# A bias row of its own for every query tile in a forgetting attention: one VectorE instruction per score block

## The chip, the cores and the metric

The kernel runs on one core of one Trainium2 chip. The time is that of the device in microseconds (us), from the first to the last instruction of the program; three runs of the kernel before gave 919.32, 919.80 and 922.17 us.

The engines are named as in the profile: PE is TensorE's matmul and PEld its weight load, DVE is VectorE, ACT is ScalarE, POOL is GpSimd, SP is SyncE, which here issues every transfer.

## The reference, cut to what matters

Eight batches of eight heads, 576 positions, 64 wide. Attention has a forgetting bias, and its output feeds a channel mix.

```python
scores = q @ k.T / sqrt(D)
cum    = cumsum(maximum(s, 0), axis=-1)
bias   = -(cum[..., :, None] - cum[..., None, :])
scores = where(causal, -1e9, scores + minimum(bias, 0))      # causal: key after query
attn   = exp(scores - max(scores)); attn = attn / (sum(attn) + 1e-9)
x      = heads side by side of attn @ v                      # [B, S, 512]
# channel mix, per position, with x_prev the position before
xk = mu_k * x + (1 - mu_k) * x_prev;  xr = mu_r * x + (1 - mu_r) * x_prev
k  = maximum(xk @ w_k, 0);  out = sigmoid(xr @ w_r) * (k * k @ w_v)
```

Within a row of scores the part of the bias that belongs to the query is a constant, and softmax does not see it. So the kernel adds only `cum` of the key, scaled by 8 (the root of D), to the raw product, the same row for every query of a head. Keys after the query get a very large negative number instead.

## The kernel before, in words

**Attention.** The 576 queries of a head are cut into five tiles: the first has 64 queries, the others 128. Tile t sees the keys up to its own last query, so its scores are 64, 192, 320, 448 and 576 columns wide (`KN`), and only the last 64 or 128 of them, from `QS[t]` on, hold keys that some query must not see. Batch 0 is done in halves so that the channel mix can begin early: `A` is tiles 0 to 2, `Z` tiles 3 and 4, for each of its four pairs of heads; from batch 1 on a visit does all five tiles (`ALL`) of a pair of heads.

`prefix_sums` puts the running sums of all 64 heads into DRAM (`cum_d`). `scores` (line 625) does one head: one transfer on SP (line 630) spreads the head's row over 128 partitions into `CB`, one of two buffers. Two selects on POOL (line 649) copy the columns that need a mask from `CB` to `M`, also one of two buffers, with the masked keys replaced: one select for the 64 columns of tile 0, one for the masked blocks of all other tiles at once. The first two heads take their rows from `first_sums`, which computes them on the spot.

For each tile `products` (line 661) makes two matmuls into one of two score banks of PSUM (line 678), and VectorE (line 693) adds the bias, scales, writes the scores to `W` and keeps the row's minimum of the negated scores in `nm`. It shows as two instructions: the pass (CUSTOM_DVE_ANT_0) and the read of the accumulator into `nm`. A tile takes two of them, the second continuing from the minimum of the first: the columns ahead of `QS[t]` with `CB`, the masked block with `M`. Tile 0 has only the masked block. Tile 4 is wider than a bank and comes as two halves of 288 columns: the first needs one pass, the second two (160 columns, then 128). ScalarE then takes exponentials and their sums (line 711), POOL normalizes (line 724), and `weighted` (line 758) transposes the weights on TensorE (line 770), copies them out with their rests (lines 797, 801, 829, 836, 844) and multiplies with the values (line 903).

Every product of 32-bit numbers is done as a rounded part and a rest. The splits of keys and queries are casts on ScalarE (lines 603, 614) and subtractions on POOL (lines 607, 618, 563), those of the weights of the channel mix lines 507 to 538.

**Channel mix.** 18 chunks of 256 positions (`channel_mix`, line 958): the mix of x and its predecessor on ScalarE and VectorE (lines 979, 988, 1007, 1011), the hidden layer (line 1040, and lines 1052 to 1069 for the square), the gate (line 1082) and the output (line 1107). The gate's result lies in one of two buffers with the tag `g`, 512 columns wide.

**The order.** No queue's order is written by hand. `Plan` collects every instruction as a task with an engine, an estimated cost, what it depends on and a due time, and simulates the five engines: on each engine the ready task that is due first goes next. It does so eight times, with due times worked back from the last simulation, keeps the shortest, and emits the instructions in that order. So the order on each queue follows from the estimated costs of all tasks; the engines then run their queues strictly in order. A buffer taken from `sbuf(shape, tag, n)` is one of n places in turn, and its tasks depend on all tasks of the place's last user. A select costs 137 ns plus 0.83 ns per column in the plan, a score pass 68 ns plus 1.04 ns per column, a transfer at least 520 ns on SP.

Of the kernel before, what the change touches and what calls it, by code (L numbers as in the profile page):

```python
# [285 lines left out]
def forgetting_attention_then_channel_mix(  # L286
# [15 lines left out]
    nc = tc.nc  # L302

    B, H, D, S = q.shape
    DM, DF = moe_w_k.shape
    P = 128
# [18 lines left out]
    def sbuf(shape, tag, bufs=1, dtype=F32):  # L325
        return plan.buffer(sb, shape, dtype, tag, bufs)

    def bank(n, tag, bufs=1):
        return plan.buffer(psum, [P, 512 * n], F32, tag, bufs)

    def fixed(t):
        b = Buffer(lambda: t)
        b.ap = t
        return b
# [7 lines left out]
    def act(emit, reads, writes, n, extra=51, table=0):  # L342
        return plan.add("ACT", n * 0.8333 + extra, emit, reads, writes, land=table)

    def dve(emit, reads, writes, n, rate=0.96):
        return plan.add("DVE", n / rate + 68, emit, reads, writes)

    def pool(emit, reads, writes, n, extra, rate=0.8333):
        return plan.add("POOL", n * rate + extra, emit, reads, writes)

    def dma(emit, reads, writes, ns):
        return plan.add("SP", max(520, ns), emit, reads, writes, land=1300)
# [13 lines left out]
    QS = [0] + [64 + P * t for t in range(NQ - 1)]  # L366
    QN = [64] + [P] * (NQ - 1)
    KN = [QS[t] + QN[t] for t in range(NQ)]
# [43 lines left out]
    cum_d = fixed(dram.tile([B * H, S], F32, name="cum_d"))  # L412
# [26 lines left out]
    def first_sums(nk):  # L439

        raw = sbuf([P, 2, nk], "raw", 4)
        ones = sbuf([P, nk], "raw", 4)
        cbs = [sbuf([P, nk], "cb", 2) for _ in range(2)]
        dma(
            lambda: nc.sync.dma_start(raw.get(), s[0:1, 0:2, 0:nk].broadcast_to([P, 2, nk])),
            [], [raw], 819 * 2 * nk / S,
        )
        pool(lambda: nc.gpsimd.memset(ones.get(), 1.0), [], [ones], nk, 36)
        act(
            lambda: nc.scalar.activation(raw.get(), raw.get(), AF.Relu, scale=ISCALE),  # L450
            [], [raw], 2 * nk, 94,
        )
        for j in range(2):
            dve(
                lambda j=j: nc.vector.tensor_tensor_scan(
                    out=cbs[j].get(), data0=ones.get(), data1=raw.get()[:, j], initial=0.0,
                    op0=ALU.mult, op1=ALU.add,
                ),
                [ones, raw], [cbs[j]], 2 * nk,
            )  # L460
        return cbs
# [83 lines left out]
    ALL, A, Z = tuple(range(NQ)), (0, 1, 2), (3, 4)  # L545
    first = []
# [78 lines left out]
    def scores(b, h, tiles, G, KH, KL):  # L625

        NK = KN[tiles[-1]]
        CB = sbuf([P, NK], "cb", 2) if not first else first.pop(0)
        (b == 0 and h < 2 and tiles == A) or dma(
            lambda: nc.sync.dma_start(  # L630
                CB.get(), cum_d.ap[b * H + h : b * H + h + 1, 0:NK].broadcast_to([P, NK])
            ),
            [cum_d], [CB], 819 * NK / S,
        )
        nm, sums, rinv = (sbuf([P, n], x, 2) for x, n in (("nm", 3 * NQ), ("sums", NQ), ("rinv", NQ)))
        if 0 in tiles:
            pool(lambda: nc.gpsimd.memset(sums.get()[:, 0:1], 1.0), [], [(sums, 0)], 1, 36)
        pt = early[h % 4] if tiles == A else weights[h % 2]


        M = sbuf([P, S], "mask", 2)

        def mask(m, k0, n):
            def own(x):
                x = x.get()[:m, k0 : k0 + n * m]
                return x if n == 1 else x.rearrange("p (t x) -> p t x", x=m)

            pool(
                lambda: nc.gpsimd.affine_select(
                    out=own(M),  # L650
                    in_=own(CB),
                    pattern=[[-1, m]] if n == 1 else [[0, n], [-1, m]],
                    base=0,
                    channel_multiplier=1,
                    compare_op=ALU.is_ge,
                    fill=MASK * ISCALE,
                ),
                [CB], [(M, k0 > 0)], n * m, 137,
            )

        def products(t, m, i, k0, w, W):
            ps = bank(1, "s", 2)
            q0 = QS[t] - QS[tiles[0]]
            if KL is None:
                r = slice(64 * (h % 2), 64 * (h % 2) + 64)
                pe(
                    lambda: nc.tensor.matmul(
                        ps.get()[:m, :w],
                        G.get()[r, q0 : q0 + m],
                        KH.get()[r, k0 : k0 + w],  # L670
                        start=True,
                        stop=True,
                    ),
                    [(G, x) for x in range(2)] + [(KH, x) for x in range(2)], [ps], w, m, 4 / 2.4, 64,
                )
            for x, K in enumerate((KH, KL) if KL is not None else ()):
                pe(
                    lambda x=x, K=K: nc.tensor.matmul(  # L678
                        ps.get()[:m, :w],
                        G.get()[:, q0 : q0 + m],  # L680
                        K.get()[:, k0 : k0 + w],
                        start=x == 0,
                        stop=x == 1,
                    ),
                    [(G, x) for x in range(2)] + [(K, x) for x in range(2)], [ps], w, m,
                )

            for a, e in ((k0, min(k0 + w, QS[t])), (max(k0, QS[t]), k0 + w)):
                if a >= e:
                    continue  # L690
                bias = CB if a < QS[t] else M
                dve(
                    lambda a=a, e=e, bias=bias, i=i: nc.vector.tensor_tensor_reduce(  # L693
                        out=W.ap[:m, a:e],
                        in0=ps.get()[:m, a - k0 : e - k0],
                        in1=bias.get()[:m, a:e],
                        scale=-SCALE,
                        scalar=3.0e38 if i == 0 else nm.get()[:m, 3 * t + i - 1 : 3 * t + i],
                        op0=ALU.add,
                        op1=ALU.min,  # L700
                        accum_out=nm.get()[:m, 3 * t + i : 3 * t + i + 1],
                    ),
                    [ps, (bias, 0 if bias is CB else t > 0)] + ([(nm, (t, i - 1))] if i else []),
                    [(W, i), (nm, (t, i))], e - a,
                )
                i += 1
            return i
# [27 lines left out]
        def rs(x):  # L735
            return x.get()[:, tiles[0] : tiles[-1] + 1]

        if 0 in tiles:
            mask(64, 0, 1)
        mask(P, QS[max(1, tiles[0])], len([t for t in tiles if t]))  # L740
        for t in tiles:
            m, n, W = QN[t], KN[t], pt[t]
            i = 0
            for k0, w in [(0, n)] if n <= 512 else [(0, n // 2), (n // 2, n // 2)]:
                i = products(t, m, i, k0, w, W)
# [3 lines left out]
                out=rs(rinv), in0=rs(sums), scalar1=1.0e-9, scalar2=None, op0=ALU.add  # L749
# [557 lines left out]
```

## Time and profile before

| | |
|---|---|
| runs | 919.32, 919.80, 922.17 us |
| median | 919.8 us |
| span of the profiled execution, which is its own time | 919.5 us |
| TensorE busy | 872.8 us, 95% |
| VectorE busy | 696.3 us, 76% |
| ScalarE busy | 693.1 us, 75% |
| GpSimd busy | 519.1 us, 56% |
| moved by transfers | 110.89 MB, mean 121 GB/s |
| mean granted clock of TensorE | 0.965 |

How to read what follows. The page gives busy times and cuts the span into 40 slices of 23 us; a digit is the busy share of a slice in tenths. A row of waits reads: engine, what it was about to do, what released it, then the total in us, how often, the longest. A row of groups reads: line, engine, operation, output and inputs with shapes, count, then busy us and mean ns of one, then idle time of the engine just before and what ended it. A matmul's end is modelled, so a busy TensorE is not one at its peak, and a weight load can wait while the matmul before it still runs.

### The profile page before, as it was taken

The numbers are of one execution on the slowest core, as the hardware profiler recorded it, in microseconds if no ns is written. First come the engines' busy times: TensorE is split into PE (matmuls) and PEld (weight loads), VectorE is DVE, ScalarE is ACT, GpSimd is POOL, SyncE is SP. The second block draws the span as 40 slices with busy tenths as digits, with TensorE's granted clock in tenths as the row PEclk, the third lists the DMA queues.
The fourth block names the chain that finished last, engine by engine and source line by source line (L and its number), as shares of the span: only waits on it lengthen the run. The fifth ranks groups of instructions, "written<-read, shape, count | busy, mean of one in ns | idle before, by whom it ended". The sixth has DMA issues, their size and how long they took to land. (4 is left out here: it accounts for less than half of the span.)

```text
span 919.5 us, 18649 instructions
## 1 busy us (share of the span) xinstructions
PE 872.8 (95%) x5546; PEld 758.6 (83%) x5546; DVE 696.3 (76%) x2473; ACT 693.1 (75%) x1834; POOL 519.1 (56%) x884
## 2 busy tenths in 40 slices
PE   6877879999999999999999999999999999998998
PEld 4656858987988898988889898989898979887886
DVE  6897998987987788778878778777787887546431
ACT  5888888998997898788968787878787876445331
POOL 6999599898576566556665646565556461100000
PEclk7568989999999999999999999999999999999999
DMA  6798645645344343434353525252434230101100
GB/s 195 223 257 237 206 123 160 174 142 168 100 151 129 109 152 87 145 112 144 100 151 93 163 61 159 79 152 79 147 97 138 79 89 25 42 31 35 46 24 23
DMA packets 65045, 110.89 MB, mean 121 GB/s; under 512 B 10544, under 2 KB 26416, under 8 KB 64944
## 3 DMA queue, kind: packets, MB, share of 16 engines
q1 hardware_dynamic: 64944, 109.71, 40.2%
q8 instruction: 43, 0.70, 0.3%
q14 instruction: 58, 0.48, 0.2%
HBM read 90.64 MB, written 19.04 MB: 119 GB/s over the span
## 5 line engine op out<-in xcount | busy, mean ns | idle before, releaser
L1040 PE MATMUL m<-xh,w_k 128*128 128x256 f32 x1152 | 231.4, 287 | 4.4 <-DVE kl L1069 4.4
L711 ACT ACTIVATE W<-W,nm 64x64 f32<-64x64 f32 (+4 forms) x320 | 179.7, 562 | 41.3 <-DVE nm L693 36.7
L770 PE MATMUL t<-ident,W 128*128 128x128 f32 (+1 forms) x960 | 188.3, 284 | 16.6 <-DVE ph L844 4.8
L1107 PE MATMUL m<-w_v,kh 128*128 128x512 f32 x576 | 198.4, 403 | 0.0
L1040 PEld LDWEIGHTS m<-xh,w_k 128*128 128x128 f32 x1152 | 186.2, 190 | 6.2 <-DVE kl L1069 4.8
L724 POOL TENSOR_SCALAR W<-W,rinv 64x64 f32<-64x64 f32 (+4 forms) x320 | 165.2, 538 | 10.6 <-DVE rinv L753 6.1
L1040 PE MATMUL m<-xl,w_k 128*128 128x256 f32 x576 | 164.6, 286 | 0.0
L770 PEld LDWEIGHTS t<-ident,W 128*128 128x128 f32 (+1 forms) x960 | 114.3, 133 | 47.5 <-DVE pl L801 7.9
L607 POOL TENSOR_TENSOR KL<-raw,KH 128x576 fp32r<-128x576 f32 (+1 forms) x72 | 98.5, 1370 | 79.8 <-ACT KH L603 73.4
L678 PE MATMUL s<-KH,G 128*128 128x288 f32 (+4 forms) x384 | 125.3, 335 | 11.3 <-ACT KH L603 5.3
L801 DVE TENSOR_TENSOR pl<-t,ph 128x256 fp32r<-128x256 f32 (+3 forms) x264 | 122.2, 472 | 16.0 <-ACT ph L797 14.7
L1107 PEld LDWEIGHTS m<-w_v,kh 128*128 128x128 f32 x576 | 106.2, 189 | 18.2 <-DVE r L530 0.2
L678 PE MATMUL s<-KL,G 128*128 128x288 f32 (+4 forms) x384 | 118.5, 312 | 2.4 <-POOL KL L607 2.4
L797 ACT CAST ph<-t 128x256 fp32r<-128x256 f32 (+3 forms) x264 | 107.3, 414 | 13.0 <-PE t L770 11.5
L1107 PE MATMUL m<-w_v,kl 128*128 128x512 f32 x288 | 117.0, 406 | 0.0
L693 DVE CUSTOM_DVE_ANT_0 W<-s,cb 128x320 f32<-128x320 f32 (+3 forms) x256 | 94.9, 375 | 26.4 <-PE s L678 21.7
L903 PE MATMUL po<-ph,V 128*128 128x448 f32 (+4 forms) x344 | 109.6, 326 | 3.7 <-ACT ph L797 1.8
L1040 PEld LDWEIGHTS m<-xl,w_k 128*128 128x128 f32 x576 | 109.2, 190 | 0.9
L618 POOL TENSOR_TENSOR G<-raw,G 64x576 fp32r<-64x576 f32 (+2 forms) x72 | 93.6, 1300 | 27.4 <-issue 13.2
L988 DVE SCALAR_TENSOR_TENSOR xp<-x,mu,xp 128x256 f32<-128x256 f32 (+3 forms) x192 | 80.4, 419 | 37.2 <-ACT xp L979 33.9
L979 ACT ACTIVATE xp<-x,mu 128x256 f32<-128x256 f32 (+3 forms) x192 | 81.5, 424 | 29.3 <-DVE xl L1011 9.7
L1082 PE MATMUL m<-w_r,xh 128*128 128x512 f32 x288 | 101.9, 407 | 0.0
(97 smaller groups left out, 1751.7 us busy)
## 6 DMA issues: line engine op xcount, KB each, us to landing
raw<-in_k SPq DMA_DIRECT2D x128, 144.0 KB, 3.2
cb<-cum_d SPq DMA_DIRECT2D x64, 288.0 KB, 3.6
raw<-in_q SPq DMA_DIRECT2D x112, 144.0 KB, 3.3
vn<-in_v SPq DMA_DIRECT2D x32, 320.0 KB, 3.8
out<-g SPq DMA_DIRECT2D x36, 256.0 KB, 2.1
x_d<-xT SPq DMA_DIRECT2D x28, 288.5 KB, 2.3
x<-x_d SPq DMA_DIRECT2D x12, 514.0 KB, 4.0
w_k<-in_moe_w_k SPq DMA_DIRECT2D x8, 512.0 KB, 5.3
```

Of the source, the lines that this page charges most:

```text
L607: lambda k=k, kh=kh, kl=kl: nc.gpsimd.tensor_tensor(out=kl.get(), in0=k.get(), in1=f32(kh.get()), op=ALU.subtract),
L678: lambda x=x, K=K: nc.tensor.matmul(ps.get()[:m, :w], G.get()[:, q0 : q0 + m], K.get()[:, k0 : k0 + w], start=x == 0, stop=x == 1,),
L693: lambda a=a, e=e, bias=bias, i=i: nc.vector.tensor_tensor_reduce(out=W.ap[:m, a:e], in0=ps.get()[:m, a - k0 : e - k0], in1=bias.get()[:m, ...
L711: lambda: nc.scalar.activation(W.ap[:m, :n], W.ap[:m, :n], AF.Exp, bias=nm.get()[:m, 3 * t + mi : 3 * t + mi + 1], scale=-1.0, accum_out=s ...
L724: lambda: nc.gpsimd.tensor_scalar(out=W.ap[:m, :n], in0=W.ap[:m, :n], scalar1=rinv.get()[:m, t : t + 1], scalar2=1.0, op0=ALU.mult, op1=AL ...
L770: lambda: nc.tensor.transpose(ps.get()[0:m, place : place + P], pt[t].ap[:, k0 : k0 + m], ident.ap),
L797: act(lambda: nc.scalar.copy(strips(ph), src()), [ps], [(ph, k) for k in ks], n * m)
L801: lambda: nc.vector.tensor_tensor(out=strips(pl), in0=src(), in1=f32(strips(ph)), op=ALU.subtract),
L903: lambda: nc.tensor.matmul(po.get()[: P if both else 64, at + q0 - base : at + q0 - base + m], V.get()[:, kb, 2 * j : 2 * j + (2 if both e ...
L1040: lambda u=u, f=f, c=c, n=n, w=w, x=x: nc.tensor.matmul(ps.get()[:, u * CT : (u + 1) * CT], weight["k", c, f // 4].get()[:, w, f % 4 * P : ...
L1082: lambda c=c, n=n, x=x, w=w: nc.tensor.matmul(ps.get(), x.get()[:, c, ts], weight["r", c, 0].get()[:, w], start=c == 0 and n == 0, stop=c ...
L1107: lambda f=f, n=n, x=x, w=w: nc.tensor.matmul(ps.get(), x.get()[:, f, ts], weight["v", f, 0].get()[:, w], start=f == 0 and n == 0, stop=f ...
```

## The change

Each head loads, for every tile of the visit, its own copy of the row, exactly as wide as that tile's keys, one beside the other in one buffer `M` of up to 1600 columns (off holds where each begins), one transfer per tile. The buffers have the tag `bias`, and there are three. POOL masks the last block of every copy in place, one select per tile, so five selects for a whole head. VectorE then takes a tile's columns in one instruction, or one for each half of tile 4. The first two heads, whose rows are computed on the spot, keep the old way: their rows now lie in places of the tag `g`, their masked blocks in a buffer of 320 columns, masked tile by tile. `mask` buffers remain only for `prefix_sums`. The scratch that the program reserves for descriptors written by software is cut to 1024 bytes; all transfers here go through SP's queue.

```diff
--- before.py
+++ after.py
@@ -440,7 +440,7 @@
 
         raw = sbuf([P, 2, nk], "raw", 4)
         ones = sbuf([P, nk], "raw", 4)
-        cbs = [sbuf([P, nk], "cb", 2) for _ in range(2)]
+        cbs = [sbuf([P, nk], "g", 2) for _ in range(2)]
         dma(
             lambda: nc.sync.dma_start(raw.get(), s[0:1, 0:2, 0:nk].broadcast_to([P, 2, nk])),
             [], [raw], 819 * 2 * nk / S,
@@ -625,37 +625,38 @@
     def scores(b, h, tiles, G, KH, KL):
 
         NK = KN[tiles[-1]]
-        CB = sbuf([P, NK], "cb", 2) if not first else first.pop(0)
-        (b == 0 and h < 2 and tiles == A) or dma(
-            lambda: nc.sync.dma_start(
-                CB.get(), cum_d.ap[b * H + h : b * H + h + 1, 0:NK].broadcast_to([P, NK])
-            ),
-            [cum_d], [CB], 819 * NK / S,
-        )
+        CB = first.pop(0) if first else None
+        off = [0]
+        for t in tiles:
+            off.append(off[-1] + KN[t])
+        M = sbuf([P, NK if CB else off[-1]], "bias", 3)
+        if not CB:
+            for t, o in zip(tiles, off):
+                dma(
+                    lambda t=t, o=o: nc.sync.dma_start(
+                        M.get()[:, o : o + KN[t]],
+                        cum_d.ap[b * H + h : b * H + h + 1, 0 : KN[t]].broadcast_to([P, KN[t]]),
+                    ),
+                    [cum_d], [(M, t)], 819 * KN[t] / S,
+                )
         nm, sums, rinv = (sbuf([P, n], x, 2) for x, n in (("nm", 3 * NQ), ("sums", NQ), ("rinv", NQ)))
         if 0 in tiles:
             pool(lambda: nc.gpsimd.memset(sums.get()[:, 0:1], 1.0), [], [(sums, 0)], 1, 36)
         pt = early[h % 4] if tiles == A else weights[h % 2]
 
 
-        M = sbuf([P, S], "mask", 2)
-
-        def mask(m, k0, n):
-            def own(x):
-                x = x.get()[:m, k0 : k0 + n * m]
-                return x if n == 1 else x.rearrange("p (t x) -> p t x", x=m)
-
+        def mask(t, m, of, at, to):
             pool(
                 lambda: nc.gpsimd.affine_select(
-                    out=own(M),
-                    in_=own(CB),
-                    pattern=[[-1, m]] if n == 1 else [[0, n], [-1, m]],
+                    out=M.get()[:m, to : to + m],
+                    in_=of.get()[:m, at : at + m],
+                    pattern=[[-1, m]],
                     base=0,
                     channel_multiplier=1,
                     compare_op=ALU.is_ge,
                     fill=MASK * ISCALE,
                 ),
-                [CB], [(M, k0 > 0)], n * m, 137,
+                [CB] if CB else [], [(M, t)], m, 137,
             )
 
         def products(t, m, i, k0, w, W):
@@ -685,22 +686,27 @@
                     [(G, x) for x in range(2)] + [(K, x) for x in range(2)], [ps], w, m,
                 )
 
-            for a, e in ((k0, min(k0 + w, QS[t])), (max(k0, QS[t]), k0 + w)):
+            o = 0 if CB else off[tiles.index(t)]
+            parts = (
+                [(CB, k0, min(k0 + w, QS[t]), 0), (M, max(k0, QS[t]), k0 + w, 0)]
+                if CB
+                else [(M, k0, k0 + w, o)]
+            )
+            for bias, a, e, o in parts:
                 if a >= e:
                     continue
-                bias = CB if a < QS[t] else M
                 dve(
-                    lambda a=a, e=e, bias=bias, i=i: nc.vector.tensor_tensor_reduce(
+                    lambda a=a, e=e, bias=bias, i=i, o=o: nc.vector.tensor_tensor_reduce(
                         out=W.ap[:m, a:e],
                         in0=ps.get()[:m, a - k0 : e - k0],
-                        in1=bias.get()[:m, a:e],
+                        in1=bias.get()[:m, o + a : o + e],
                         scale=-SCALE,
                         scalar=3.0e38 if i == 0 else nm.get()[:m, 3 * t + i - 1 : 3 * t + i],
                         op0=ALU.add,
                         op1=ALU.min,
                         accum_out=nm.get()[:m, 3 * t + i : 3 * t + i + 1],
                     ),
-                    [ps, (bias, 0 if bias is CB else t > 0)] + ([(nm, (t, i - 1))] if i else []),
+                    [ps, (bias, 0 if bias is CB else t)] + ([(nm, (t, i - 1))] if i else []),
                     [(W, i), (nm, (t, i))], e - a,
                 )
                 i += 1
@@ -735,9 +741,11 @@
         def rs(x):
             return x.get()[:, tiles[0] : tiles[-1] + 1]
 
-        if 0 in tiles:
-            mask(64, 0, 1)
-        mask(P, QS[max(1, tiles[0])], len([t for t in tiles if t]))
+        for t, o in zip(tiles, off):
+            if CB:
+                mask(t, QN[t], CB, QS[t], QS[t])
+            else:
+                mask(t, QN[t], M, o + QS[t], o + QS[t])
         for t in tiles:
             m, n, W = QN[t], KN[t], pt[t]
             i = 0
@@ -1276,7 +1284,7 @@
     import concourse.bacc as bacc
     from concourse.bass_utils import run_bass_kernel_spmd
 
-    nc = bacc.Bacc("TRN2", target_bir_lowering=False, num_devices=1)
+    nc = bacc.Bacc("TRN2", target_bir_lowering=False, num_devices=1, dynamic_dma_scratch_size=1024)
     arrays, args = {}, []
     for name in _INS:
         a = inputs[name]
```

## The prediction, made before the result was known

> **What bounds the kernel now.** I read the page first (busy shares and the span in slices), then three stretches of the span, then the waits of TensorE, then the groups by shape on VectorE and GpSimd, last the transfers.
>
> ```profile
> span 919.5 us, 18649 instructions
> ...
> PE 872.8 (95%) x5546; PEld 758.6 (83%) x5546; DVE 696.3 (76%) x2473; ACT 693.1 (75%) x1834; POOL 519.1 (56%) x884
> ...
> PE   6877879999999999999999999999999999998998
> ...
> DVE  6897998987987788778878778777787887546431
> ...
> POOL 6999599898576566556665646565556461100000
> PEclk7568989999999999999999999999999999999999
> ```
> ```profile
> 0.00:161.00 161.00, 128.69 (x682) 101.24 (x683) 138.38 (x480) 129.24 (x344) 137.44 (x235) 0.80 0.68 200
> 161.00:830.00 669.00, 660.94 (x4382) 585.08 (x4381) 521.70 (x1934) 532.06 (x1432) 381.64 (x650) 1.00 0.38 113
> 830.00:919.50 89.50, 83.13 (x487) 72.30 (x485) 36.21 (x61) 31.84 (x60) 0.00 (x0) 1.00 0.10 33
> ```
> ```profile
> 46.00:69.00 23.00, 18.24 (x72) 13.11 (x71) 22.46 (x81) 19.57 (x55) 20.98 (x36) 0.65 0.90 256
> 69.00:92.00 23.00, 17.85 (x108) 14.49 (x107) 17.98 (x56) 18.91 (x47) 21.53 (x29) 0.83 0.87 237
> ...
> 115.00:138.00 23.00, 16.14 (x89) 12.50 (x89) 22.78 (x87) 20.62 (x55) 22.17 (x31) 0.85 0.40 123
> ```
>
> The columns of the stretches are length, then busy time of TensorE, its weight loads, VectorE, ScalarE and GpSimd, then granted clock, DMA share and GB/s. There are three stages. Until 161 us TensorE idles 32 of 161 us and its granted clock averages 0.80; VectorE (138.4) and GpSimd (137.4) are both busy some 86% of it, and in 115 to 138 us both are above 96%. From 161 to 830 us TensorE is busy 661 of 669 us at clock 1.00, so it is the bound, and VectorE is at 78%, GpSimd at 57%. The tail is the channel mix alone, which the change does not touch. So the change can be worth something in the first stage, where two engines are near their limit, and in the second only through short gaps on TensorE. Those gaps stand in the waits:
>
> ```profile
> PEld s L678 <- DVE nm L693: 13.0, 28, 1.2
> ...
> PEld t L770 <- DVE pl L801: 7.9, 20, 0.8
> ...
> PEld t L770 <- DVE pl L836: 7.2, 13, 1.5
> ...
> PEld t L770 <- POOL W L724: 6.7, 13, 1.0
> ...
> PE s L678 <- DVE nm L693: 5.3, 12, 1.1
> ```
> ```profile
> PEld s L678 <- DVE nm L693: 8.6, 20, 1.2
> PEld t L770 <- DVE pl L801: 5.8, 16, 0.8
> PEld t L770 <- DVE pl L836: 3.0, 6, 0.8
> ```
>
> The first fence is the whole run, the second 161 to 830 us. TensorE or its weight loads wait for VectorE to free a score bank 18.3 us in all, and for VectorE's transposed rests some 15 us more. A weight load that waits is not all lost time, since the matmul before it may still run; it is an upper bound of what a quicker VectorE gives back.
>
> **The change, part by part.**
>
> VectorE:
>
> ```profile
> L693 DVE CUSTOM_DVE_ANT_0 W<-s,mask,nm 128x128 f32<-128x128 f32 x256 | 86.9, 343 | 3.5 <-DVE nm L693 0.2
> ...
> L693 DVE DVE_READ_ACCUMULATOR2_ANT nm<- 128x1 f32 x576 | 46.6, 81 | 0.0
> ...
> L693 DVE CUSTOM_DVE_ANT_0 W<-s,cb 128x320 f32<-128x320 f32 x64 | 31.0, 484 | 2.4 <-PE s L678 2.1
> ...
> L693 DVE CUSTOM_DVE_ANT_0 W<-s,cb 128x192 f32<-128x192 f32 x64 | 22.5, 351 | 6.6 <-PE s L678 5.3 <-PE t L770 0.9
> ```
>
> Each score instruction is a pair: the pass itself and an accumulator read of 81 ns. From 192 to 320 columns the pass grows by 133 ns. Where a tile's masked block is now a second pass (343 + 81 = 424 ns), it becomes 128 more columns of the first (133 ns): 291 ns saved, and the same in the half tile of the last query tile, whose other half is unmasked anyhow. A head with all five tiles loses 4 of 10 pairs; a head of an early or late half of batch 0 loses 2 of 5; the first two heads keep the old form. That is 56 x 4 + 6 x 2 + 8 x 2 = 252 pairs, 73 us of VectorE's 696. Before 161 us there are 120 pairs (6 early halves, 8 late ones and 4 whole heads with the new form), of which 44 go: 12.8 us of 138.4. The other 60.5 us lie in the second stage, where VectorE falls from 78% to 69%.
>
> What of it lies on the path in the second stage: the bank of a 320-column tile is held 484 + 81 + 343 + 81 = 989 ns, then 698, about 30% less. The 8.6 us of waits for a bank fall at least by those 30% (2.6 us), at most wholly. The 8.8 us for transposed rests queue behind VectorE's other work and fall with its load, a tenth to a half (1 to 4 us). Bounds 0 (another wait fills each gap) and 17.4 us (all three rows); the parts give 3.5 to 12.6, and I take 5.5 us, towards the low side, because a waiting weight load hides partly behind a running matmul.
>
> GpSimd:
>
> ```profile
> L649 POOL TENSOR_SCALAR_AFFINE_SELECT mask<-cb 128x512 f32<-128x512 f32 x56 | 35.5, 634 | 0.0
> ...
> L649 POOL TENSOR_SCALAR_AFFINE_SELECT mask<-cb 128x256 f32<-128x256 f32 x16 | 6.5, 409 | 1.0 <-DMA cb<-cum_d 0.9
> ```
> ```profile
> 0.00:161.00 161.00, 12.34 (x34) 0.80 0.68 200
> ```
>
> The same 512 columns are masked in four selects in place of one. Between 256 and 512 columns the cost grows 225 ns, 0.88 ns per column, so a select has 184 ns that does not shrink: 3 more selects cost 552 ns per whole head, 1 more 184 ns per half head. The last row is line 649 alone: 34 selects before 161 us, that is 16 and 8 for the half heads and 10 for five whole heads. There 8 + 8 + 15 = 31 more stand, 5.7 us on 137.4. In the second stage 28 us are added to 382 of 669: covered, as GpSimd idles 43%. In the first stage the cover is thin: the selects stand in one queue with the rests of the keys and queries, the weights' rests and the normalizing, and TensorE's weight loads wait for the normalized W 6.7 us over the run. The VectorE gain of 12.8 us and the GpSimd loss of 5.7 us work on two engines that are equally full, so the fuller one goes from 138.4 to 143.1, while the two wait less for one another. Bounds there: -12.8 (VectorE alone decides) to +5.7 (GpSimd alone decides); I take 0, between, nearer to GpSimd's row, since GpSimd is then the fuller engine.
>
> Transfers:
>
> ```profile
> q1 hardware_dynamic: 64944, 109.71, 40.2%
> ...
> cb<-cum_d SPq DMA_DIRECT2D x64, 288.0 KB, 3.6
> ...
> mu<-in_moe_mu_k SPq DMA_DIRECT2D x1, 2.0 KB, 1.8
> ```
> ```profile
> SPq L630 <- DVE nm L693: 144.4, 46, 9.5
> ```
> ```profile
> L630 SPq DMA_DIRECT2D cb<-cum_d x70: 319/326/571, 18.7 to 754.3; - x70
> ```
> ```profile
> POOL mask L649 <- DMA cb<-cum_d: 2.6, 3, 1.0
> ```
>
> A whole head loads 64 + 192 + 320 + 448 + 576 = 1600 columns in five transfers instead of 576 in one, an early half 576 instead of 320, a late half 1024 instead of 576. That is 32 MB and 31,232 packets more on 109.7 MB and 64,944: by bytes the share of 40% becomes 52%, by packets 60%. SyncE issues 4 more at 326 ns, 1.3 us per whole head. Queued behind them on SyncE are the loads of queries, keys and values, and ScalarE's and GpSimd's splits wait for those. SyncE already stands 144 us at this line until VectorE has done with the buffer; with three buffers in place of two the load goes out a head earlier, so the 2.6 us that selects wait for their rows should not grow; a select that does wait holds up the rests and the normalizing behind it on GpSimd. After 161 us (share 0.38) I take 0; bounds 0 and, if each of five rows is as often late as the one is now and TensorE feels all of it, 5 x 2.6 = 13 us. Before 161 us see the last rival.
>
> Moving the first two rows to buffers of the gate, and the smaller scratch, issue nothing: 0. All queues' orders are rebuilt by the planner from its own costs, which no row prices; I leave that to the range.
>
> Sum, on the profiled execution's span of 919.5 us (0.3 us under the median of the runs): 919.5 - 5.5 + 0 + 0 = 914.0 us.
>
> **A rule against it.** The row says that 288 KB land in 3.6 us and 2 KB still take 1.8. The Trainium skill, "DMA: Bandwidth & Descriptors", section "Rules for kernel authors", says to coalesce many small transfers, as under 64 KB one pays mostly overhead; the 64-column piece is 32 KB. The trace agrees that small ones are not cheap; by that rule the packets count, not the bytes, and the time would be that of the last rival, 927, not 914.
>
> **The rivals.**
>
> VectorE alone sets the first stage. For it: 22.46 and 22.78 of 23 us in 46 to 69 and 115 to 138. Against: 17.98 in 69 to 92, where GpSimd has 21.53. Half of the 12.8 us come back: 919.5 - 5.5 - 6.4 = 907.6 us; all of it gives 901.
>
> Nothing comes of it: the last query tile takes two instructions still, the rest is quicker where nobody waits, since in the second stage TensorE is busy 99% and the waits are hidden behind running matmuls; in the first the two engines balance. 919.5 us.
>
> GpSimd becomes the bound of the first stage, which ends on the slower side. It is the next engine at 137.4 of 161, every added select stands ahead of a split or a normalize in its queue, and TensorE's weight loads wait for W. All 31 selects count: 919.5 + 5.7 = 925.2 us. It decides if the second stage gives back less than 2.9 us (5.7 less the 2.8 that can be told). Against: GpSimd itself idles 23 us of that stage.
>
> The transfers of the first stage fill the engines. In 46 to 92 us the share is 0.90 and 0.87, 40.7 of 46 us. The late halves carry 0.23 MB more each; at 109.71 MB in 40.2% of 919.5 us (0.297 MB/us) six of them add 4.6 us, which fills the stretch, and whole heads loaded ahead (0.52 MB more, 1.8 us each) overflow it, two to four of them by 3.5 to 7 us. Weights and keys then come that late: 923 to 927 us. Against: the weights are asked for well ahead of use.
>
> **How the numbers follow.** Chances: the forecast 0.37, VectorE alone 0.16, nothing 0.21, GpSimd 0.16, transfers 0.10. A measurement here tells 0.3%, 2.8 us, from no change. Faster 0.37 + 0.16 = 0.53, same 0.21, slower 0.26. The range 904 to 926 us leaves out the full VectorE gain below and the worse half of the transfers above; the bounds all on one side (919.5 - 17.4 - 12.8 = 889 and 919.5 + 5.7 + 13 + 7 = 945) would need every part to go one way. For the forecast alone the range is 909 to 917.
>
> **What would show it.** Right: the pairs of line 693 fall from 640 to 388 and VectorE's busy time by some 73 us; GpSimd's rises by some 34 us (56 x 552 + 16 x 184 ns); waits of line 678 for VectorE fall from 18.3 to about 11 us; the DMA share rises to 52 to 60%; the stretch to 161 us holds as much TensorE work as before. Wrong: selects that wait long for their rows, weight splits that wait for transfers before 115 us, more TensorE idle than 32 us in the first stage, or a TensorE gap in the second that no part of the change explains, which would be the new order of the queues.

## The result, and the profile after

The changed kernel takes 979.64 us (median of four runs, 978.81 to 980.49) against 919.56 before: ratio 1.0646, 95% interval 1.0629 to 1.0663. The forecast was 914.0 in a range of 904 to 926. The profiled execution took 978.81 us, its span is 977.0.

The page of the changed kernel, its head and the chain of work that ended last:

```profile
span 977.0 us, 18947 instructions
...
PE 887.1 (91%) x5546; PEld 771.7 (79%) x5546; DVE 662.7 (68%) x1969; ACT 691.4 (71%) x1834; POOL 545.5 (56%) x1068
...
PE 47%; DMA 21%; ACT 13%; DVE 9%; issue 5%; POOL 3%; SPq 1%; POOLq 0%; ACTq 0%; DVEq 0%
PE m L1048 17%; PE m L1115 8%; DMA x<-x_d 8%; PE m L1090 6%; PE t L778 5%; PE s L679 5%; PE po L911 4%; DMA bias<-cum_d 4%; ACT xp L987 4%; DMA raw<-in_k 4%; ACT W L717 3%; DVE xp L996 3%; DVE W L699 2%; POOL W L730 1%; DMA raw<-in_q 1%
```

The span grew by 57.5 us. TensorE does the same 5546 matmuls; it idles 89.9 us (977.0 less 887.1) where it idled 46.7, and its matmuls take 14.3 us longer. A fifth of the chain is now transfers, and most of that is not the new rows (4%) but x, keys and queries (13%). The three stretches, columns as in the prediction:

```profile
0.00:161.00 161.00, 120.73 (x595) 95.20 (x596) 121.73 (x354) 115.67 (x308) 126.47 (x238) 0.70 0.72 212
161.00:830.00 669.00, 625.54 (x4132) 553.45 (x4131) 474.77 (x1485) 515.97 (x1401) 416.29 (x826) 0.98 0.51 155
830.00:977.00 147.00, 140.84 (x824) 123.03 (x822) 66.18 (x131) 59.75 (x126) 2.79 (x6) 0.99 0.10 33
```

At 161 us 595 matmuls are done in place of 682, at 830 us 4727 in place of 5064: the loss runs through the first two stages. In the first, the granted clock is 0.70 in place of 0.80. The second stage, where TensorE was busy 661 of 669 us, now has 43 us of gaps. What they wait for, over the whole run:

```profile
POOL bias L650 <- DMA bias<-cum_d: 75.4, 64, 2.7
...
ACT xp L987 <- DMA x<-x_d: 39.1, 16, 5.1
...
PEld s L679 <- DVE nm L699: 31.0, 34, 4.4
...
PE s L679 <- DVE nm L699: 20.4, 19, 4.2
```

The selects' wait for their rows, 2.6 us before, is 75.4. TensorE's two rows of waits for a score bank, which were to fall from 18.3 to 11 us, rose to 51.4. The transfers of the changed kernel by kind, with KB each and the median time from issue to landing, and then the key loads of the kernel before:

```profile
q1 hardware_dynamic: 100080, 141.71, 47.5%
...
raw<-in_k SPq DMA_DIRECT2D x128, 144.0 KB, 6.5
bias<-cum_d SPq DMA_DIRECT2D x64, 288.0 KB, 7.5
...
x<-x_d SPq DMA_DIRECT2D x12, 514.0 KB, 6.6
...
bias<-cum_d SPq DMA_DIRECT2D x62, 32.0 KB, 4.7
```
```profile
raw<-in_k SPq DMA_DIRECT2D x128, 144.0 KB, 3.2
```

A key load, which the change does not touch, lands after 6.5 us in place of 3.2. The added bytes are the 32 MB that the prediction counted, the added packets 35,136 in place of its 31,232 (144 for each of the 244 loads, not 128); the share is 47.5%, below the 52 to 60% it gave. Transfers got slow while their engines were not full.

One gap from near, from the timeline of the changed kernel. Each row has the start, the length, engine, line and operation; the bracket holds the idle time before and what ended it:

```profile
314.91 0.37 ACT L987 ACTIVATE xp<-x,mu 128x128 f32<-128x128 f32 x1 [3.69 <-DMA x<-x_d]
...
315.32 0.36 DVE L996 SCALAR_TENSOR_TENSOR xp<-x,mu,xp 128x128 f32<-128x128 f32 x1 [2.79 <-ACT xp L987]
...
316.34 0.29 POOL L650 TENSOR_SCALAR_AFFINE_SELECT bias<-bias 128x128 f32<-128x128 f32 x1 [1.87 <-DMA bias<-cum_d]
...
318.23 0.19 PEld L679 LDWEIGHTS s<-KH,G 128*128 128x128 f32 x1 [2.16 <-DVE nm L699]
```
```profile
308.23 0.56 SPq L1140 DMA_DIRECT2D x<-x_d  x1
308.84 0.67 SPq L636 DMA_DIRECT2D bias<-cum_d  x1
...
314.95 7.91 SPq L636 DMA_DIRECT2D bias<-cum_d  x5
323.95 0.47 SPq L588 DMA_DIRECT2D raw<-in_k  x1
```

The second fence is SyncE's queue there. x is asked for at 308.23 and lands just before 314.91, 6.7 us later. ScalarE waits 3.7 us for it, VectorE, whose queue has the mix next, 2.8 us for ScalarE, and the score passes behind that mix are late, so that TensorE finds no free bank for 2.2 us. SyncE then stands at five bias loads for 7.91 us. Issuing them takes 1.67 us of that; four of them go out 0.02 us after the VectorE pass that frees their place (over the run SyncE waits 49.4 us here for VectorE). So late passes delay the next loads in turn, and the keys behind them go out at 323.95.

VectorE did not save what was forecast. Its queue in the kernel before, then in the changed one:

```profile
301.35 0.48 DVE L693 CUSTOM_DVE_ANT_0 W<-s,cb 128x320 f32<-128x320 f32 x1
301.76 0.08 DVE L693 DVE_READ_ACCUMULATOR2_ANT nm<- 128x1 f32 x1
301.76 0.34 DVE L693 CUSTOM_DVE_ANT_0 W<-s,mask,nm 128x128 f32<-128x128 f32 x1
302.03 0.08 DVE L693 DVE_READ_ACCUMULATOR2_ANT nm<- 128x1 f32 x1
302.03 0.69 DVE L1062 SCALAR_TENSOR_TENSOR m<-m,r 128x512 f32<-128x512 f32 x1
```
```profile
302.86 0.62 DVE L699 CUSTOM_DVE_ANT_0 W<-s,bias 128x448 f32<-128x448 f32 x1
303.41 0.08 DVE L699 DVE_READ_ACCUMULATOR2_ANT nm<- 128x1 f32 x1
303.52 0.30 DVE L945 TENSOR_TENSOR xT<-t,xT 64x128 f32<-64x128 f32 x1
```

The same tile of 448 columns. The read starts 0.07 us before its pass ends, and the next pass starts with the read. Two pairs hold VectorE from 301.35 to 302.03, 0.68 us, and the one from 302.86 to 303.41, 0.55 us. A pair less is worth 0.13 us of the engine, not the 0.291 that the sum of its two rows gives. Over the run VectorE's busy time fell by 33.6 us for 252 pairs, 0.133 each.

### The profile page after: what moved, and what is told of

It reads as the page before. It is cut to its first block, busy times and chain, and to the rows that moved or that the text cites. A ratio compares the mean times of both kernels' runs of the same rounds, so it can differ in the third digit from the quotient of the medians.

```text
span 977.0 us, 18947 instructions
## 1 busy us (share of the span) xinstructions
PE 887.1 (91%) x5546; PEld 771.7 (79%) x5546; DVE 662.7 (68%) x1969; ACT 691.4 (71%) x1834; POOL 545.5 (56%) x1068
## 2 busy tenths in 40 slices
DMA packets 100183, 142.90 MB, mean 146 GB/s; under 512 B 22384, under 2 KB 61552, under 8 KB 100080
## 3 DMA queue, kind: packets, MB, share of 16 engines
q1 hardware_dynamic: 100080, 141.71, 47.5%
## 4 chain that ended last, share of the span: by engine, by line
PE 47%; DMA 21%; ACT 13%; DVE 9%; issue 5%; POOL 3%; SPq 1%; POOLq 0%; ACTq 0%; DVEq 0%
PE m L1048 17%; PE m L1115 8%; DMA x<-x_d 8%; PE m L1090 6%; PE t L778 5%; PE s L679 5%; PE po L911 4%; DMA bias<-cum_d 4%; ACT xp L987 4%; DMA raw<-in_k 4%; ACT W L717 3%; DVE xp L996 3%; DVE W L699 2%; POOL W L730 1%; DMA raw<-in_q 1%
## 5 line engine op out<-in xcount | busy, mean ns | idle before, releaser
L1048 PE MATMUL m<-xh,w_k 128*128 128x256 f32 x1152 | 239.6, 292 | 2.5 <-DVE kl L1077 2.5
L778 PE MATMUL t<-ident,W 128*128 128x128 f32 (+1 forms) x960 | 197.3, 290 | 34.2 <-DVE pl L844 10.9
L1048 PEld LDWEIGHTS m<-xh,w_k 128*128 128x128 f32 x1152 | 192.8, 195 | 4.4 <-DVE kl L1077 2.8
L778 PEld LDWEIGHTS t<-ident,W 128*128 128x128 f32 (+1 forms) x960 | 118.0, 135 | 66.3 <-DVE pl L844 17.6
L1048 PE MATMUL m<-xl,w_k 128*128 128x256 f32 x576 | 167.4, 291 | 0.0
L699 DVE CUSTOM_DVE_ANT_0 W<-s,bias 128x288 f32<-128x288 f32 (+4 forms) x316 | 129.7, 423 | 36.8 <-PE s L679 25.1
L650 POOL TENSOR_SCALAR_AFFINE_SELECT bias<-bias 128x128 f32<-128x128 f32 (+1 forms) x314 | 80.9, 278 | 90.5 <-DMA bias<-cum_d 75.4
L911 PE MATMUL po<-ph,V 128*128 128x448 f32 (+4 forms) x344 | 114.0, 338 | 13.9 <-ACT ph L805 11.4
L1048 PEld LDWEIGHTS m<-xl,w_k 128*128 128x128 f32 x576 | 112.2, 195 | 0.7
L679 PEld LDWEIGHTS s<-KH,G 128*128 128x128 f32 (+1 forms) x384 | 74.4, 195 | 45.9 <-DVE nm L699 31.0
```

The costliest lines, as they stand in the source:

```text
L679: lambda x=x, K=K: nc.tensor.matmul(ps.get()[:m, :w], G.get()[:, q0 : q0 + m], K.get()[:, k0 : k0 + w], start=x == 0, stop=x == 1,),
L699: lambda a=a, e=e, bias=bias, i=i, o=o: nc.vector.tensor_tensor_reduce(out=W.ap[:m, a:e], in0=ps.get()[:m, a - k0 : e - k0], in1=bias.get( ...
L778: lambda: nc.tensor.transpose(ps.get()[0:m, place : place + P], pt[t].ap[:, k0 : k0 + m], ident.ap),
L911: lambda: nc.tensor.matmul(po.get()[: P if both else 64, at + q0 - base : at + q0 - base + m], V.get()[:, kb, 2 * j : 2 * j + (2 if both e ...
L1048: lambda u=u, f=f, c=c, n=n, w=w, x=x: nc.tensor.matmul(ps.get()[:, u * CT : (u + 1) * CT], weight["k", c, f // 4].get()[:, w, f % 4 * P : ...
```

## The experiments

All ratios are to the kernel before, run beside it on the same chip, with 95% intervals. In the diffs, `r` is the head's row.

**Loads alone, VectorE left as before.** *b_five_loads* is the kernel before, every queue in its order of before, with the change's added loads, which nothing reads.

```diff
+ for t in tiles[:-1]:
+     nc.sync.dma_start(extra.get()[:, o : o + KN[t]],
+         cum_d.ap[r : r + 1, 0 : KN[t]].broadcast_to([P, KN[t]]))
```

> The kernel before, every other engine's queue in its old order; each bias load is followed at once by the four (early half two, late half one) further loads of the change, into a buffer that nobody reads. So it adds the transfers of the change and nothing else. Transfers theory (the added packets make every other load land late, and engines stall on loads): the landing of keys goes from 3.2 to about 6 us and the time to 950 to 980 us. Order theory (the loads are harmless; the queue order that the planner builds from the new tasks is what costs): 917 to 925 us, landings up by at most 1 us.

Measured: 1054.57 us, 1.1446 (1.1417 to 1.1474), far above both ranges; the keys land after 7.7 us. The added loads alone cost 133 us, more than twice the whole loss, in an order that does not know of them.

*b_one_extra_load* takes one added load of the same bytes in place of the four.

```diff
+ nc.sync.dma_start(extra.get()[:, 0:w],   # w: the sum of the four widths
+     row.rearrange("(o x) -> o x", o=1).broadcast_to([P, w]))
```

> The kernel before in its old order, with the same added bytes as in the change but as one more load per head, 128 rows of 1024 columns (early half 256, late half 448). Transfers theory by number of packets or of loads: close to before, 919 to 930 us; transfers theory by bytes: as slow as with four added loads, 950 us or more. Order theory: 917 to 923 us.

Measured: 953.25 us, 1.0355 (1.0313 to 1.0398). The time lies just inside the range given for bytes, but it is not as slow as with four loads: 32 us, where the same bytes in 244 loads cost 133. So the price does not go with the bytes alone. Per load it is 0.46 and 0.55 us, which looks like a price for each load; the runs on place below show that this need not be so.

**VectorE's part alone.** *a_one_row* has the changed kernel's instructions in its order, with one row of 576 columns per head loaded for all tiles and masked in place. It leaves out the other four loads, so that a tile finds parts of its bias masked wrongly.

```diff
- lambda t=t, o=o: nc.sync.dma_start(M.get()[:, o : o + KN[t]], ...)
+ lambda t=t: t == tiles[0] and nc.sync.dma_start(M.get(), ...[r, 0:NK])
```

> The changed kernel with every other engine's queue in the order of the changed kernel, but each head loads one row as wide as its last tile, as before the change; all tiles read their bias from it and mask their block in it, so the other loads are left out, and masks of one tile stand in the next one's bias (part of the bias is masked that should not be). One VectorE instruction per block and five selects stay. Transfers theory: the landings return to 3 to 4 us and the time to 905 to 925 us. Order theory: 965 to 980 us, though landings are short.

Measured: 915.34 us, 0.9934 (0.9915 to 0.9954). Its first two stretches:

```profile
0.00:161.00 161.00, 130.89 (x700) 105.24 (x700) 133.67 (x393) 129.62 (x347) 140.32 (x266) 0.79 0.71 201
161.00:830.00 669.00, 658.13 (x4399) 584.22 (x4398) 496.22 (x1527) 532.07 (x1438) 402.83 (x803) 1.00 0.39 114
```

And its waits, over the whole run:

```profile
PEld s L678 <- DVE nm L698: 13.6, 26, 1.7
...
PE s L678 <- DVE nm L698: 6.0, 11, 1.4
...
POOL bias L649 <- DMA bias<-cum_d: 2.9, 5, 1.1
```

Without the added loads the rest of the change gains 5.8 us against 921.18 beside it. TensorE is 18 matmuls ahead of the kernel before at 161 us and 35 at 830. The waits for a bank did not fall (19.6 us against 18.3).

**The planner.** *a_land_6us* tells the plan that a transfer lands after 6 us.

```diff
- return plan.add("SP", max(520, ns), emit, reads, writes, land=1300)
+ return plan.add("SP", max(520, ns), emit, reads, writes, land=6000)
```

> The changed kernel with the planner told that a transfer lands 6.0 us after its issue in place of 1.3 us, near the medians of the changed profile; all work is the same, only the order of the queues is new. If the order is slow because selects and splits stand in their queues before their loads can have landed, the waits of selects for loads (75 us) fall below 30 us and the time to 930 to 960 us. If the transfers themselves are too much, it stays at 965 us or more.

Measured: 959.1 us, 1.0408 (1.0383 to 1.0433). The time is just inside the first range, but its reason did not come: selects still wait 68.8 us for rows, not below 30. The new order recovers a third of the loss; it does not make the loads quick (the keys land after 6.7 us).

**Number, width or place.** *b_five_narrow* is b_five_loads with each added load 64 columns wide. *b_five_distinct* has the widths of b_five_loads, and each of the 128 partitions reads a row of its own, of the keys.

```diff
+ nc.sync.dma_start(extra.get()[:, o : o + 64], cum_d.ap[r : r + 1, 0:64].broadcast_to([P, 64]))  # narrow
+ nc.sync.dma_start(extra.get()[:, o : o + KN[t]], <128 rows of k>[:, 0 : KN[t]])                  # distinct
```

> The kernel before in its old order with four added loads per whole head as in the changed kernel's number, but each only 64 columns wide (256 bytes for each of 128 partitions, all from one place in DRAM), into a buffer that nobody reads. One-place theory (a load that spreads one row over 128 partitions holds the queue about 1.5 us however narrow, since all partitions read the same place) and per-load theory (each load has a fixed price, eight in flight): 1000 to 1055 us, as with the full widths (1052). Bytes theory: below 935 us.

> The kernel before in its old order with four added loads per whole head of the full widths (64, 192, 320, 448 columns), but their 128 rows come from 128 different places (rows of the keys) instead of one row of the running sums; nobody reads them. One-place theory: much faster than the 1052 us of the same loads from one row, 925 to 970 us. Per-load theory and bytes theory: 1030 us or more.

Measured: narrow 1043.11 us, 1.1333 (1.1307 to 1.1358); distinct 945.41 us, 1.0267 (1.0239 to 1.0294). A quarter of the added bytes (8.0 MB in place of 32.0) changes little; other places with all the bytes take away four fifths of the price. The 25 us that stay are near the 32 of b_one_extra_load, which adds the same bytes, so those 32 us may be bytes rather than a price for each load. *a_distinct* does the same to the changed kernel: all its loads and its order, with the rows of keys as sources, so that the forgetting bias is left out of the result.

> The changed kernel, same queues, same number and widths of loads, but the 128 partitions of each bias load read 128 different rows (of the keys) instead of one row of the running sums, so the bias is not the right one: the forgetting part is left out. One-place theory: the price of the loads falls from some 62 us (977 against 915 with one row) to about that of the distinct loads in the old order (25 us), 925 to 950 us, and the keys' landing to 4 to 5 us. Per-load or bytes theory: 965 us or more.

Measured: 919.67 us, 0.9994 (0.998 to 1.0008), even below the range expected. 60 us of the loss go with the place alone. Its transfers:

```profile
q1 hardware_dynamic: 100080, 141.71, 53.0%
...
raw<-in_k SPq DMA_DIRECT2D x128, 144.0 KB, 3.8
bias<-in_k SPq DMA_DIRECT2D x64, 288.0 KB, 4.0
```

Packets and bytes are those of the changed kernel to the last digit, and the keys land after 3.8 us in place of 6.5. *b_narrow_spread* is b_five_narrow with one difference: its partitions read 128 places that follow one another.

```diff
- cum_d.ap[r : r + 1, 0:64].broadcast_to([P, 64])
+ cum_d.ap.rearrange("r x -> (r x)")[0 : P * 64].rearrange("(p x) -> p x", p=P)
```

> The kernel before in its own queue order, with four added loads per visit as in b_five_narrow: 64 columns each, 128 partitions, 32 KB, read by nothing. The one difference to b_five_narrow: the 128 partitions of a load read 128 places that follow one another in DRAM (32 KB in one piece), not all the same 256 bytes. Theory (one place read by all partitions is what costs): most of the price goes, 922 to 940 us, and the raw key loads land within about 4.5 us. Rival (small rows cost, or the number of loads): at least 1030 us, near b_five_narrow's 1043, key loads landing near 7.5 us. Anything between 950 and 1020 would say that both count.

Measured: 925.63 us, 1.0052 (1.0033 to 1.0072). The transfers of b_five_narrow and then of b_narrow_spread:

```profile
q1 hardware_dynamic: 100080, 117.72, 37.7%
...
raw<-in_k SPq DMA_DIRECT2D x128, 144.0 KB, 8.2
...
extra<-cum_d SPq DMA_DIRECT2D x244, 32.0 KB, 6.5
```
```profile
q1 hardware_dynamic: 100080, 117.72, 44.3%
...
raw<-in_k SPq DMA_DIRECT2D x128, 144.0 KB, 3.0
...
extra<-cum_d SPq DMA_DIRECT2D x244, 32.0 KB, 3.0
```

The same queue order, the same 100,080 packets and 117.72 MB, and 117 us apart. 244 small loads from many places cost 5 us; from one place each they cost 123. The engines' busy time is no larger in the slow one (37.7% of 1043.0 us are 393 us, 44.3% of 924.1 are 409): the time lies where this profile shows nobody busy. From the landings in the two traces, such a load lands 1.67 us (median) after the one issued before it in b_five_narrow, and 0.18 us in b_narrow_spread. In b_five_loads, rows of 256, 768, 1280 and 1792 bytes give 1.47, 1.76, 1.98 and 1.66 us: it hardly goes with the width, and is 11 to 15 ns for each of the 128 readers.

The packets of 256 bytes are no slower themselves (median 15 ns in b_five_narrow, 18 in b_narrow_spread). What differs is how many are in work at once: 1.6 on average over the time with any, against 5.0. It is not that few engines carry such a load: in b_five_loads the packets of 1792 bytes, also from one place, reach 18 at once.

The changed kernel itself shows where the price lies. From the narrowest to the widest, the five loads of a head land 0.27, 1.49, 1.58, 1.90 and 1.62 us (medians) after the transfer issued before them; with the sources of a_distinct it is 0.19, 0.47, 0.76, 0.75 and 1.24. The first, which mostly follows a transfer of another kind, adds little to it, and at 2304 bytes a row most of the distance is there from separate places too. The loads in the middle, right behind a load of the same row, pay most.

**Versions that keep the result, with fewer loads.** *a_downwards*: one row, tiles from last to first, each block masked in place just before its use. *a_one_wide_load*: the five rows lie side by side in DRAM and come in one load of 1600 columns. *a_two_sides*: the row twice in one load, downwards, tiles alternating between the two copies.

```diff
+ for t in tiles[::-1]:                                  # downwards
+     mask(t, QN[t], M, QS[t], QS[t])
+ M.get(), cum_d.ap[r : r + 1, a : a + w]...             # one_wide_load, w = 1600
+ mask(t, QN[t], M, side[t] * NK + QS[t], ...)           # two_sides, side 0 or 1
```

> One row of 576 columns per head in three buffers, one VectorE instruction per block, and the tiles taken from the last to the first: each tile masks its block in place after the tile behind it has been read, so no further copies are needed and the result is the reference's. It has the loads of before and VectorE's gain of 73 us, but five selects that each wait for VectorE. Transfers theory: 905 to 925 us; if the chain of selects and VectorE within a head sets the pace, 930 us or more.

> The changed kernel with the five rows of a head laid side by side in DRAM (1600 columns) and loaded as one transfer of 6400 bytes for each partition: the bytes of the change, the number of transfers of before, otherwise the change. One-place and per-load theories: 925 to 955 us, as the one added load of the same bytes cost 32 us in the order of before. Bytes theory: 970 us or more.

> One load per head of the row twice (1152 columns), tiles from the last to the first in turn on either copy, each masked in place after the tile two before it has been read; one VectorE instruction per block, result the reference's. Against one copy (926.8 us) the chain of selects and VectorE is half as tight, against the wide load (927.4) it moves 1152 in place of 1600 columns: 912 to 924 us. If chain and bytes do not matter: 925 us or more.

Measured: 926.83 (1.0078, 1.0048 to 1.0108), 927.39 (1.0075, 1.0051 to 1.0099) and 922.46 us (1.0011, 0.9999 to 1.0022). Each takes back nearly all of the loss and none is faster than before. The first lies between its two ranges, the other two inside the first of theirs. The first and the third let a select wait for the passes that read its block before; that this is their price was not tested, nor what the wide load pays for.

**Fewer loads than before.** *b_pair_row* loads the rows of both heads of a pair at once, *b_pair_last* also masks the last tile in the row itself and gives it one instruction less.

```diff
+ CB = sbuf([P, 2, NK], "cb", 2)   # both: one load for heads h and h + 1
+ [(k0, k0 + w)] if t == tiles[-1] else ...   # b_pair_last
```

> The kernel before with one bias load for both heads of a visit (two rows side by side, 4608 bytes for each partition; two buffers of two rows) in place of one per head: 34 loads in place of 70, same bytes, two VectorE instructions per block as before. One-place theory: a load that spreads one row holds the queue some 1.5 us whatever its width, so halving the loads helps the first 160 us: 908 to 918 us. If only added loads cost and the 70 are hidden: 917 to 923 us.

> As the version with one load for both heads, and the last tile of a visit is masked in place in the row (no other tile reads these columns), so its last block takes one VectorE instruction: 72 pairs fewer, 21 us of VectorE, 72 selects more, 13 us of GpSimd, no load more. If VectorE's gain is worth what it was with one row (252 pairs gave 4 to 6 us): 1 to 3 us under the version with one load for both heads. If the added selects outweigh it: equal or slower.

Measured: 924.98 us, 1.0049 (1.0035 to 1.0063), and 923.26 us, 1.0023 (1.0012 to 1.0033). Halving the loads of before (35 in place of 70) is worth nothing: the time is above both ranges. At one load per head the selects wait only 2.6 us for it. The second is 1.7 us under the first, as expected of its 72 pairs. Both were given a new order by the plan, so that this is not shown to be VectorE's gain, and why they are a little slower than before is open.

**VectorE's part with no added load.** *b_wide_select_late* lets GpSimd copy, masking on the way, whole rows of tiles 0 to 3 from the one loaded row, from batch 2 on.

```diff
- own(CB) -> own(M)                                      # 64 + 512 columns
+ CB.get()[:m, 0:n] -> M.get()[:m, off[t] : off[t] + n]  # per tile, 1152 columns in all
```

> The kernel before with its one load per head. From batch 2 on GpSimd's selects copy, for each of tiles 0 to 3, all columns of the tile out of the one loaded row into a buffer of 1024 columns with the block masked on the way; tile 4 is masked in the loaded row itself. VectorE then takes a tile, or a half of tile 4, in one instruction, as in the changed kernel. No transfer is added. GpSimd's selects of a head take 5 instructions over 64+192+320+448+128 = 1152 columns in place of 576: about 1.9 us in place of 0.85, so some 1.06 us x 48 heads = 51 us more of GpSimd's busy time, all after the first stage where it is busy 57%. Theory (the loss is in the added loads, and what VectorE saves is worth its 5 to 6 us where GpSimd has room): 912 to 917 us. Rival (GpSimd's longer selects are late for the scores, or hold up splits and normalizing behind them): 920 to 928 us.

Measured: 934.73 us, 1.0143 (1.0121 to 1.0165), above both ranges. Its page and first two stretches:

```profile
PE 877.8 (94%) x5547; PEld 761.3 (82%) x5547; DVE 671.0 (72%) x2089; ACT 692.7 (74%) x1834; POOL 561.3 (60%) x1028
```
```profile
0.00:161.00 161.00, 125.46 (x655) 98.72 (x656) 136.53 (x468) 126.46 (x337) 135.82 (x235) 0.79 0.69 201
161.00:830.00 669.00, 656.00 (x4349) 578.84 (x4349) 492.48 (x1549) 529.85 (x1428) 425.48 (x794) 1.00 0.38 113
```

VectorE fell by 25.3 us for 192 pairs, 0.132 each, as above. But TensorE is 27 matmuls behind already at 161 us, before the first edited instruction (195 us) has run: the plan had put all queues in another order. How much of the loss is that order and how much the longer selects is open.

## Why the prediction was wrong

**The transfers term failed**, the step "the load goes out a head earlier, so the 2.6 us that selects wait for their rows should not grow", taken as 0 and bounded by 13 us. It was sized by bytes, packets, issue time and engine share; the bytes came out as said, the packets an eighth higher, the share lower. What it left out is in b_narrow_spread against b_five_narrow: among loads that stand in a row, one whose 128 partitions read one place costs the queue 1.5 to 2.0 us between 256 and 1792 bytes a row, and everything behind it on SyncE's one queue lands later. The loads of a head, asked for one after another, are such loads. A head earlier did not help, because the term is a rate: with 244 more of them, each load of keys and x came about 3 us later. In every trace transfers land in the order in which they were issued, and at most eight are in flight, so slow loads also hold back the issue of later ones: SyncE waits 85.7 us for landings in the changed kernel, 4.4 before and 17.8 in a_distinct. By the ratios, each to the kernel before beside it, the term is 65.5 us (a_one_row to the changed kernel): 60 are the place alone, and 5.5 (a_one_row to a_distinct) the number and the bytes.

**The last rival** named the right part and the wrong cause. It expected the engines to fill up in the first stage, at 923 to 927 us; the share there is 0.72, and the loss runs on through the second stage.

**The rule weighed there**, coalescing in the Trainium skill, "DMA: Bandwidth & Descriptors", section "Rules for kernel authors", would have made the small pieces dear; it speaks of the size of a transfer, and that the packets then set the time was the prediction's own step. It does not fit: 244 loads of 32 KB cost 5 us in b_narrow_spread, and 70 loads of mostly 512 KB cost 32 us. b_five_narrow, with the same small loads from one place, decides for the place. The Trainium skill, "SBUF — State Buffer", section "A bandwidth-pool intuition that's wrong (but worth ruling out)", gives a port of the memory 22.5 GB/s. 32 KB in 1.47 us would be 22 GB/s; but 224 KB in 1.66 us are 138, so one port for a whole row is ruled out. For each 256 bytes of the row, the four widths give 22, 19, 17 and 20 GB/s, so a limit on every such piece is not. Which part serves one place so slowly stays open, and so does whether it is the repeated address or the way the load is written (a step of 0 between partitions); no run shows it.

**The VectorE term was mis-sized.** 640 pairs became 388, as said, but busy time fell by 33.6 us, not 73: 0.13 us per pair, because rows that overlap were added up. **The gain on the path**, forecast at 5.5 us, was 5.8 in a_one_row. That agrees in size and not in place, and so is luck as far as the runs show: the bank waits it was drawn from did not fall, about half the lead arises in the first stage, where 0 was taken, and a_one_row has the plan's new order as well, so that it isn't shown to be VectorE's time.

**GpSimd** rose by 26.4 us, not 34, and in a_one_row, with all added selects, TensorE is ahead of the kernel before at 161 us. That rival fell. With the price of the one place gone, "Nothing comes of it" would have been the best guess: a_distinct has 0.9994.

## What to carry to other kernels

Before adding a broadcast load, ask how many partitions read the same bytes and how many such loads stand in a row: here each behind another cost the queue 1.5 to 2.0 us between 256 and 1792 bytes a row, and one of 256 bytes a tenth of that from separate places, while halving the one load per head of before gained nothing. Read the price of a transfer from how far apart landings lie when several are queued, not from the bytes, the engines' share or the landing time of one that has the queue to itself. Price an instruction by the distance between the starts of neighbours in the timeline, since the durations of a group overlap.

## What was not expected of the hardware

- One place read by 128 partitions: 1.67 us between landings against 0.18 us for 128 neighbouring places, at 256 bytes each, while the transfer engines are busy no longer (393 against 409 us).
- Transfers that read other memory are held up with them: the keys land after 8.2 us against 3.0.
- A pass of VectorE and the read of its accumulator overlap: the read of 81 ns starts 74 ns (median) before its pass ends, and a split tile costs 0.13 us more than a whole one, not 0.29.
- In the first stage, where TensorE idled 40 us in place of 32, its granted clock was 0.70 in place of 0.80; over the run the same 5546 matmuls took 14.3 us longer.
